# A gated mix of two attentions: maxima 90 slots ahead instead of 96, and two orders of halves in the projections

## The chip, the cores and the metric

One core of a Trainium2 chip runs the whole program. The time is device microseconds of one execution, the median of several runs. PE is the matrix engine, DVE the vector engine, ACT the scalar engine, POOL the general engine, SP the queue that issues most transfers.

## What is computed

`x` has 2048 rows of 512. Attention A is plain softmax attention with 32 heads of 16; attention B is causal-type attention within four chunks of 512 rows (the mask adds -1e9 where the key's row stands before the query's), mixed with a memory summed over the chunks before. A gate per row mixes both results. Cut to the core:

```python
qkv = split_heads(x @ wqkv)                                  # A
p = softmax(q @ k.T * scale); a = merge(p @ v) @ wo
for s in range(4):                                           # B, chunk by chunk
    p = softmax(qs @ ks.T * scale + mask); a_dot = p @ vs
    a_mem = (phi(qs) @ M) / (phi(qs) @ z + 1e-6)
    o[s] = sigmoid(beta) * a_mem + (1 - sigmoid(beta)) * a_dot
    M += phi(ks).T @ vs; z += phi(ks).sum()
b = merge(o) @ wo
out = g * a + (1 - g) * b        # g = sigmoid(x . gate_w)
```

## The kernel before

The program is written out in a fixed order for each engine; nothing is reordered later. It has a front and a slot loop.

**Front.** Projections are run in "slots" of twelve products of 128x512 (2 to 3 us of PE). Each operand is split into a high half (a rounded copy, ACT) and a low half (the rest, a subtraction on DVE or POOL), and a product is made of three half products. Work of the other engines is posted at one of four places in a slot: `post_at(n, place, f)` in slot n, `post(d, place, f)` d slots after the present one. What is posted at the same place runs in the order of posting. The slots are: 0 and 1 the values' first products (their additions, L550, follow on DVE, and the banks that they read come free); 2 and 3 take the split of the query weights (`wq8`, tile `qtmp` the low half, cast from `ph`); eight query tiles follow (`qk_tile`: copy L428, high half L429, low half L437, two stores to `qdA`); then the rest of the values; then the keys of two chunks in `k_pair`, seven slots with two accumulators each (copy L484, addition L491/L497/L502, high half L473, low half L477, stores to `kdA`), and again for the other two chunks; then values and, from slot 50 on, B's queries and keys with the memory (`tps`, `mps`, `num`, `den`).

**Maxima.** A score needs the row maximum of its query row in advance: the product is made once for the maximum alone (L242, into a bank `sm`), DVE reduces it over 512 columns (L275 for A; L290 with the mask for B), POOL combines the parts, PE transposes them (L232, `mt_ps`), ACT copies (L235, `mt`), and SP writes them as extra rows into the query tile (L238), so that the second product (L1065, `st`) gives scores less their maximum. A list `maxs` fixes the order of all 2368 maxima, with B's spread between A's. Those of the first `LEAD` slots are made in the front, four at a time (`some_max`), between projection tiles.

**Slot loop.** There are 2368 slots: 31 times a unit of A (64 slots) and one of B (10), then B31 and A31. A unit is four heads by 512 queries; A30 is the last A unit but one. Slot n makes one score (L1065), its exponential on ACT (L1088), and, `LEAD` slots ahead, one maximum. Three slots are a burst; at its end come products with values (L155, `ops`) or the transposition of maxima, whichever is due. A transposition becomes due 9 slots behind the last maximum of the next A unit or 12 slots ahead of the unit's own first score, whichever is first; two that are due together share one bank and one ACT copy. At the end, when no maxima are left (`wide`, `LEAD` - 6 slots), banks of the maxima serve scores too, six slots make a group, and output products fill PE (`fill`, up to 11 less the values taken): 24 for one block of rows, then the last chunk's (`blk`, `qclosed`, `kA` reused).

Of the kernel before, what the change touches and what calls it, by code (L numbers as in the profile page):

```python
# [31 lines left out]

SLOTS = {"A": 64, "B": 10}
NU = 32
LEAD = 96
BURST = 3
LATER = (2, 3)
MOST = 3
# [9 lines left out]
def gated_mix(ctx, tc, x, xT, wqkv, a_wo, b_wq, b_wk, b_wv, b_wo, beta, gate_w, out):  # L48
# [52 lines left out]
    def unit(side, k):  # L101
        return side, k % NG, k // NG
# [15 lines left out]
    for k in range(NU):  # L118
        mine = {u: iter(range(32)) for u in range(2)}
        bs = [k - 1] if 0 < k < NU - 1 else [k - 1, k] if k else []  # L120
        theirs = {r: [(unit("B", b), (r, i)) for b in bs for i in range(5)] for r in range(2)}
        start, apart = (33, (3, 3)) if k == 1 else (6, (9, 3)) if k < NU - 1 else (23, (3, 3))
        at_ = [next(m for m in range(len(maxs) + start, len(maxs) + start + 6) if m % 3 == 0)]
        while len(at_) < 10 * len(bs):
            at_.append(at_[-1] + apart[len(at_) % 2])
        for m in range(len(maxs), len(maxs) + 64 + 10 * len(bs)):
            r = (m + 1) % 2
            if m in at_ and bs:
                maxs.append(theirs[r].pop(0))
            else:  # L130
                maxs.append((unit("A", k), (r, next(mine[r]))))
        assert not theirs[0] and not theirs[1]
    last_max = {u: m for m, (u, _) in enumerate(maxs)}
    a_last = sorted(last_max["A", k % NG, k // NG] for k in range(NU))
    first_max = {u: m for m, (u, _) in reversed(list(enumerate(maxs)))}
    assert len(maxs) == nS and all(first[u] + LEAD - last_max[u] > 24 for u in units)

    qt, kt_ = {}, {}

    def raw(t):  # L140

        return t[:].bitcast(F32)
# [14 lines left out]
    def wait_early(n):  # L157

        loads_ = []
        for m in range(n + 1 + LEAD, n + 1 + BURST + LEAD):  # L160
            if m < nS:
# [47 lines left out]
    def finish_max(u):  # L209
        nm = pmt.pop(u)  # L210
        if u[0] == "A":
            pm, nm = nm, mp.tile([128, 4, 4], F32, tag="nm", name="nm")
            dm = mp.tile([128, 4, 4, 2], F32, tag="dm", name="dm")
            nc.gpsimd.tensor_sub(dm, pm[:, :, :, 2:4], pm[:, :, :, 0:2])  # L214
            nc.gpsimd.tensor_scalar_min(dm, dm, 0.0)
            nc.gpsimd.tensor_add(dm, dm, pm[:, :, :, 0:2])
            nc.gpsimd.tensor_sub(nm, dm[:, :, :, 1], dm[:, :, :, 0])
            nc.gpsimd.tensor_scalar_min(nm, nm, 0.0)
            nc.gpsimd.tensor_add(nm, nm, dm[:, :, :, 0])

        ms = mp.tile([128, 2, 2, 2, 4], F32R, tag="ms", name="ms")
        nv = nm.rearrange("p (r h) s -> p r h s", r=2)
        nc.gpsimd.tensor_copy(ms[:, :, 0], nv)  # L223
        nc.gpsimd.tensor_sub(ms[:, :, 1], nv, ms[:, :, 0].bitcast(F32))
        return ms
# [37 lines left out]
    def max_part(m, bank, b=None):  # L263
# [34 lines left out]
        if m == last_max[u]:  # L298
            def finish():

                due = min(e for e in a_last if e >= last_max[u]) + LATE_T
                late.append((min(due, first[u] + LEAD - 12), u, finish_max(u)))
            todo.append((m + 1, finish))

    def run_todo(m):

        for e in [e for e in todo if e[0] <= m]:
            todo.remove(e)
            e[1]()
# [22 lines left out]
    mnext = [0]  # L332
    with ExitStack() as p0:
# [22 lines left out]
        def f32(t):  # L356
            t = t[:]
            return t if t.dtype == F32 else t.bitcast(F32)
# [17 lines left out]
        def post(slots, place, f):  # L376
            posted.setdefault((now[0] + slots, place), []).append(f)
# [3 lines left out]
        def slot(products=(), chained=False):  # L381

            for place in range(4):
                for ps, l, r, start, stop in products[3 * place:3 * place + 3]:
                    nc.tensor.matmul(ps, l, r, start=start, stop=stop, skip_group_check=chained)  # L385
                for f in posted.pop((now[0], place), []):
                    f()
            now[0] += 1
# [6 lines left out]
        def post_at(n, place, f):  # L395
            posted.setdefault((n, place), []).append(f)
# [3 lines left out]
        def split(hi, lo, src, eng=V):  # L400

            nc.scalar.copy(hi, f32(src))
            eng.tensor_sub(lo, f32(src), f32(hi))
# [57 lines left out]
        def k_pair(xo, cs):  # L461

            X, Y, t = [None] * 2, [None] * 2, {}

            def out_tile(o, c, full, g, eng):
                q1 = wk.tile([128, CH], F32R, tag="q1", name="q1", bufs=3)
                q2 = wk.tile([128, CH], F32R, tag="q2", name="q2", bufs=3)

                def store(i, q):
                    nc.sync.dma_start(kd["A", o, cs[c]][16 * i:16 * i + 16].rearrange("d h t -> (d h) t"), raw(q))  # L470

                def high():
                    nc.scalar.copy(q1, full)  # L473
                    store(0, q1)

                def low():
                    eng.tensor_sub(q2, full, q1.bitcast(F32))  # L477
                    store(1, q2)
                post(*((0, 2) if g == 0 else (1, 0)), high)
                post(*((0, 3) if g == 0 else (1, 1)), low)  # L480

            def copy_x(g, tag):
                full = wk.tile([128, CH], F32, tag=tag, name="full", bufs=2)
                nc.scalar.copy(full, X[g])  # L484
                return full

            def done(p, g):
                if p == "p1":
                    t["1", g] = copy_x(g, "full")
                elif p == "p2":  # L490
                    V.tensor_add(t["1", g], Y[g], t["1", g])  # L491
                    out_tile(g, 0, t["1", g], g, V)
                elif p == "p6":
                    t["a", g] = copy_x(g, "am")
                elif p == "p5":
                    t["5", g] = copy_x(g, "full")
                    V.tensor_add(t["5", g], Y[g], t["5", g])  # L497
                    out_tile(2 + g, 1, t["5", g], g, V)
                elif p == "p3":
                    out_tile(2 + g, 0, copy_x(g, "full"), g, V)  # L500
                elif p == "p4":
                    V.tensor_add(t["a", g], Y[g], t["a", g])  # L502
                    out_tile(g, 1, t["a", g], g, V)
            for p, x, w in ORDER:
                x, w = xo[x], kops[w]
                prods = []
                for g in range(2):
                    if p == "p1":
                        X[g] = sm_bank()
                    elif p in ("p2", "p7"):  # L510
                        Y[g] = me_bank() if p == "p2" else pr_bank()
                    first = p in ("p1", "p2", "p7")
                    ps = X[g] if p in ("p1", "p6", "p5", "p3") else Y[g]
                    prods += [(ps, w[a][k][:, 128 * g:128 * g + 128], x[b][k], first and (a, b, k) == (1, 0, 0), (a, b, k) == (0, 0, 1))
                              for k in range(2) for a, b in PARTS]
                    post(0, 1 + 2 * g, lambda p=p, g=g: done(p, g))
                slot(prods, not first)
# [73 lines left out]
        def raw_ph():  # L591
            return [wk.tile([128, CH], F32, tag="ph", name="ph", bufs=4) for _ in range(4)]
# [23 lines left out]
        qraw = raw_ph()  # L616
# [3 lines left out]
        wq8 = (K4[1], Q4[0])  # L620
# [12 lines left out]
            op_split(vops["21" if k > 1 else "11"], vr[0][k // 2 * 2:], V, [k % 2])  # L633
            op_split(xo0["12" if k > 1 else "11"], x0[k // 2 * 2:], V, [k % 2])
        for k in range(KT):
            post_at(2, k, lambda k=k: split(wq8[0][k], wq8[1][k], qraw[k]))
            post_at(4, k, lambda k=k: op_split(xo0["22"] if k > 1 else a21, x1[k // 2 * 2:], V, [k % 2]))
        vb = (vr[0][0:2], vr[1][0:2], vr[0][2:4], vr[1][2:4])
        for k in range(2):
# [240 lines left out]
        def some_max():  # L880
            m = mnext[0]
            if m == LEAD:
                return
            loads(m + 3 + PRE)
            for i in range(4):
                max_part(m + i, lambda: me_sm.tile([128, CH], F32, tag="sm", name="sm"))
            run_todo(m + 3)
            mnext[0] += 4
            run_late(me_ps, "me", mnext[0])

        post_at(36, 1, lambda: loads(16))
# [8 lines left out]
        for n in range(32):  # L900
            if n in (14, 21, 29):
                post_at(S0 + n, 3, lambda c=n // 8: mem_q(c))
            elif n in (2, 4, 6, 8, 10, 12, 16, 18, 22, 24, 26):
                post_at(S0 + n, 3, some_max)

        def gates():
# [133 lines left out]

    wide = range(nS - LEAD + 2, nS - 4)
    assert wide.start % (2 * BURST) == wide.stop % (2 * BURST) == 0
# [115 lines left out]
    def octet(side, o, c, t0, vector=False):  # L1158
# [67 lines left out]
        if t0 is not None:  # L1226

            t0 += max([e + 2 - LEAD - t0 - ts[1] for e in a_last if 0 <= e + 1 - LEAD - t0 - ts[1] < 12], default=0)
        for n, f in zip(ts, (load, factors, send, factor, scale, store)):
# [117 lines left out]
    n = 0  # L1347
    while n < nS or queue or beside or filled[0] < len(fill):
# [4 lines left out]
        m = n + LEAD  # L1353
# [81 lines left out]
```

## Time and profile before

| | us |
|---|---|
| median of 3 runs (1738.92 to 1739.48) | 1738.96 |
| the profiled execution | 1738.98 |
| its span, first to last instruction | 1737.10 |
| front, to the first score | 272.7 |
| slots with maxima | 1389.2 |
| slots without maxima, to the last score | 51.5 |
| behind the last score | 23.8 |

Busy shares of the span: PE 100%, DVE 93%, ACT 83%, POOL 41%. PE's records are pipelined and their ends are modelled, so its share does not tell what it could still take; what it does is read from the starts of its rows. In the lines of the profile, `L242` is line 242 of the kernel, `sm<-kA,qA` says what is written from what, `x4` that four such instructions are merged, and `[0.84 <-DVE vs L550]` that the engine was idle 0.84 us until that instruction was done.

### The profile page before, as it was taken

The numbers are of one execution on the slowest core, as the hardware profiler recorded it, in microseconds if no ns is written. First come the engines' busy times: TensorE is split into PE (matmuls) and PEld (weight loads), VectorE is DVE, ScalarE is ACT, GpSimd is POOL, SyncE is SP. The second block draws the span as 40 slices with busy tenths as digits, with TensorE's granted clock in tenths as the row PEclk, the third lists the DMA queues.
The fourth block names the chain that finished last, engine by engine and source line by source line (L and its number), as shares of the span: only waits on it lengthen the run. The fifth ranks groups of instructions, "written<-read, shape, count | busy, mean of one in ns | idle before, by whom it ended". The sixth has DMA issues, their size and how long they took to land.

```text
span 1737.1 us, 41522 instructions
## 1 busy us (share of the span) xinstructions
PE 1729.1 (100%) x15157; PEld 875.5 (50%) x15157; DVE 1608.8 (93%) x3376; ACT 1439.9 (83%) x2774; POOL 706.8 (41%) x964
## 2 busy tenths in 40 slices
PE   9999999999999999999999999999999999999998
PEld 7877775444444444444444444444444444444444
DVE  7777987999999999999999999999999999999931
ACT  6543667888888888888888888888888888888884
POOL 1022544233353437444535353435354353435442
PEclk9999999999999999999999999999999999999999
DMA  7679887435453446454444453445444444444542
GB/s 246 193 241 238 303 278 218 112 93 156 116 159 102 142 124 175 132 141 125 137 138 143 133 148 122 134 140 139 141 123 149 131 141 113 144 119 147 149 152 63
DMA packets 168651, 264.97 MB, mean 153 GB/s; under 512 B 39512, under 2 KB 80760, under 8 KB 168448
## 3 DMA queue, kind: packets, MB, share of 16 engines
q1 hardware_dynamic: 166720, 260.78, 50.5%
q8 instruction: 121, 1.98, 0.5%
q0 software_dynamic: 1440, 1.14, 0.3%
q14 instruction: 82, 0.67, 0.1%
q10 hardware_dynamic: 288, 0.39, 0.1%
HBM read 177.74 MB, written 83.25 MB: 150 GB/s over the span
## 4 chain that ended last, share of the span: by engine, by line
PE 97%; DVE 1%; DMA 1%; ACT 0%; SPq 0%; issue 0%; ACTq 0%; DVEq 0%
PE ops L155 40%; PE st L1065 28%; PE sm L242 14%; PE pr L385 9%; PE pair L385 2%; PE sm L155 2%; DMA u<-xT 0%; PE mt_ps L232 0%; PE tps L851 0%; PE sm L1065 0%; DVE pm L275 0%; DMA u<-x 0%; PE mps L865 0%; PE num L823 0%; PE den L827 0%
## 5 line engine op out<-in xcount | busy, mean ns | idle before, releaser
L1088 ACT ACTIVATE p<-st 128x512 f32<-128x512 f32 x2261 | 1190.7, 600 | 146.8 <-PE sm L242 93.3
L275 DVE TENSOR_REDUCE pm<-sm 128x1 f32<-128x512 f32 x2048 | 1276.2, 682 | 8.3 <-PE sm L242 7.6
L242 PE MATMUL sm<-kA,qA 48*128 48x512 f32 x2048 | 662.2, 424 | 0.0
L1065 PE MATMUL st<-qA,kA 50*128 50x512 f32 x2014 | 655.9, 431 | 0.0
L155 PE MATMUL ops<-p,vA 128*17 128x256 f32 (+3 forms) x6360 | 552.2, 445 | 0.0
L1065 PEld LDWEIGHTS st<-qA,kA 50*128 50x128 f32 x2014 | 326.9, 185 | 423.4 <-ACT p L1088 379.7
L242 PEld LDWEIGHTS sm<-kA,qA 48*128 48x128 f32 x2048 | 337.8, 185 | 11.0 <-issue 4.2
L1189 POOL TENSOR_TENSOR rcp<-rec,minus 128x32 f32<-128x32 f32 x43 | 234.8, 5461 | 75.8 <-DMA rec<-dend 71.2
L290 DVE CUSTOM_DVE_ANT_0 rest<-sm,mask 128x128 f32<-128x128 f32 (+3 forms) x512 | 246.5, 481 | 0.0
L155 PEld LDWEIGHTS ops<-p,vA 128*17 128x17 f32 x6360 | 129.1, 96 | 215.7 <-issue 184.5
L1069 POOL TENSOR_SCALAR_AFFINE_SELECT p<-p 128x512 f32<-128x512 f32 x128 | 79.6, 638 | 267.6 <-ACT p L1088 263.1
L242 PE MATMUL sm<-kB,qB 48*128 48x128 f32 (+3 forms) x512 | 166.1, 384 | 0.0
L1065 PE MATMUL st<-qB,kB 50*128 50x512 f32 (+1 forms) x495 | 105.3, 329 | 0.3 <-ACT mt L235 0.3
L385 PE MATMUL pr<-u,u 128*128 128x512 f32 x392 | 101.4, 397 | 0.0
L1065 PEld LDWEIGHTS st<-qB,kB 50*128 50x128 f32 x495 | 68.5, 186 | 62.2 <-ACT p L1088 50.4
L155 PE MATMUL ops<-p,vB 128*17 128x128 f32 (+3 forms) x1504 | 88.3, 350 | 0.0
L385 PEld LDWEIGHTS pr<-u,u 128*128 128x128 f32 x392 | 71.8, 188 | 19.0 <-ACT u L834 2.5
L242 PEld LDWEIGHTS sm<-kB,qB 48*128 48x128 f32 x512 | 79.9, 184 | 0.0
L214 POOL TENSOR_TENSOR dm<-pm 128x32 f32<-128x32 f32 x32 | 7.8, 245 | 170.9 <-DVE pm L275 170.9
L434 POOL TENSOR_SCALAR mn<-full 128x512 f32<-128x512 f32 x24 | 39.0, 1625 | 53.8 <-ACT full L428 53.7
L223 POOL CAST ms<-pm 128x16 fp32r<-128x16 f32 x32 | 6.3, 198 | 127.5 <-DVE pm L290 127.5
L1205 POOL TENSOR_TENSOR v<-v,inv 128x512 f32<-128x512 f32 x31 | 39.8, 1284 | 28.7 <-DMA inv<-rdA 21.7
(227 smaller groups left out, 1422.5 us busy)
## 6 DMA issues: line engine op xcount, KB each, us to landing
kA<-kdA SPq DMA_DIRECT2D x256, 128.0 KB
vA<-vdA SPq DMA_DIRECT2D x31, 544.0 KB
kA<-kdA SPq DMA_DIRECT2D x256, 64.0 KB
kB<-kdB SPq DMA_DIRECT2D x192, 64.0 KB
qB<-qdB SPq DMA_DIRECT2D x192, 64.0 KB
kdA<-q SPq DMA_DIRECT2D x32, 256.0 KB
qA<-qdA SPq DMA_DIRECT2D x64, 128.0 KB
qdB<-q SPq DMA_DIRECT2D x32, 256.0 KB
```

Of the source, the lines that this page charges most:

```text
L155: behind[0] = nc.tensor.matmul(*args, **kw)
L214: nc.gpsimd.tensor_sub(dm, pm[:, :, :, 2:4], pm[:, :, :, 0:2])
L242: nc.tensor.matmul(ps[:, n0:n0 + n], rows(qt[u][:, :, s * 128:(s + 1) * 128], h, 48), rows(k[:, :, k0:k0 + n], h, 48), start=True, stop=True)
L275: nc.vector.tensor_reduce(pm[:, h, s, kc:kc + 1], ps, axis=AX.X, op=ALU.max, negate=True)
L290: nc.vector.tensor_tensor_reduce(out=tri["rest"][:, 0:w], in0=ps[:, n0:n0 + w], in1=tri["mask"][:, CH - w:], scale=-1.0, scalar=3.0e38, op ...
L385: nc.tensor.matmul(ps, l, r, start=start, stop=stop, skip_group_check=chained)
L434: nc.gpsimd.tensor_scalar_min(ph["mn"], full, 0.0)
L1065: nc.tensor.matmul(ps[:, n0:n0 + CH - q0], rows(k[:, :, b * 128:(b + 1) * 128], h, 50), rows(q[:, :, q0:], h, 50), start=True, stop=True)
L1069: nc.gpsimd.affine_select(out=x, in_=x, pattern=[[0, 4], [1, 128]], base=0, channel_multiplier=-1, compare_op=ALU.is_ge, fill=0.0)
L1088: nc.scalar.activation(p[:, h], ps, AF.Exp, scale=SCALE)
L1189: eng.tensor_tensor(r, rec, minus, op=ALU.pow)
L1205: eng.tensor_mul(k["v"], k["v"], k["inv"])
```

## The change

Four edits: the lead of the maxima falls from 96 to 90 slots, with B0's and the last B units' places in the list moved by six so that they meet the same slots as before; the front makes 90 maxima in 23 calls, the last one of two, instead of 96 in 24 (the calls in slots 60 and 62 become one in 61); the split of the third and fourth query weight moves from slot 2 to slot 3; and in `k_pair` the high half is made one place later, behind the next accumulator's copy, and the low half behind it.

```diff
-LEAD = 96
+LEAD = 90
...
-        start, apart = (33, (3, 3)) if k == 1 else (6, (9, 3)) if k < NU - 1 else (23, (3, 3))
+        start, apart = (27, (3, 3)) if k == 1 else (6, (9, 3)) if k < NU - 1 else (17, (3, 3))
...
-                post(*((0, 2) if g == 0 else (1, 0)), high)
-                post(*((0, 3) if g == 0 else (1, 1)), low)
+                post(*((0, 3) if g == 0 else (1, 2)), high)
+                post(*((1, 0) if g == 0 else (1, 3)), low)
...
-            post_at(2, k, lambda k=k: split(wq8[0][k], wq8[1][k], qraw[k]))
+            post_at(2 + k // 2, k, lambda k=k: split(wq8[0][k], wq8[1][k], qraw[k]))
...
-            for i in range(4):
+            for i in range(min(4, LEAD - m)):
                 max_part(m + i, lambda: me_sm.tile([128, CH], F32, tag="sm", name="sm"))
-            run_todo(m + 3)
-            mnext[0] += 4
+            run_todo(min(m + 3, LEAD - 1))
+            mnext[0] = min(m + 4, LEAD)
...
-            elif n in (2, 4, 6, 8, 10, 12, 16, 18, 22, 24, 26):
+            elif n in (2, 4, 6, 8, 11, 16, 18, 22, 24, 26):
```

On DVE at the end of the values' first products, the low halves of the query weights (`qtmp`) and the additions of values (`vs`):

```order
 L403 TENSOR_TENSOR u_257<-u_246,u_257 128x512
 L403 TENSOR_TENSOR qtmp<-ph,kA_194 128x512 x2
-L403 TENSOR_TENSOR qtmp<-ph,kA_195 128x512 x2
-L550 TENSOR_TENSOR vs<-pr,vt 128x8x4x16 x4
+L550 TENSOR_TENSOR vs<-pr,vt 128x8x4x16 x2
+L403 TENSOR_TENSOR qtmp<-ph,kA_195 128x512
+L550 TENSOR_TENSOR vs<-pr,vt 128x8x4x16
+L403 TENSOR_TENSOR qtmp<-ph,kA_195 128x512
+L550 TENSOR_TENSOR vs<-pr,vt 128x8x4x16
 L403 TENSOR_TENSOR kA_193<-u_247,kA_192 128x512 x2
```

The first addition stood behind four low halves and stands behind two; the other two low halves stand between additions.

On ACT in the first `k_pair`, copies of accumulators (`full<-pair`) and high halves (`q<-full`):

```order
 L402 CAST u_946<-ph 128x512 x2
-L484 COPY full<-pair 128x512
+L484 COPY full<-pair 128x512 x2
 L473 CAST q_954<-full 128x512
 L484 COPY full<-pair 128x512
-L473 CAST q_969<-full 128x512
+L402 CAST qtmp<-u_600 128x512 x2
+L473 CAST q_967<-full 128x512
+L484 COPY full<-pair 128x512
+L473 CAST q_981<-full 128x512
```

Both copies now stand ahead of the high half that stood between them.

On PE behind the last maximum, first of before, then of now: the groups of six scores (`st` and `sm` from `qA`, `qB`), values (`ops`), transpositions (`mt_ps`) and output products (`blk`):

```order
L1065 MATMUL st<-qA_21624,kA_195 128x512 x3
L1065 MATMUL sm_3246<-qA_21624,kA_195 128x512
L1065 MATMUL sm_3247<-qA_21624,kA_195 128x512
L1065 MATMUL sm_3248<-qA_21624,kA_195 128x512
L155 MATMUL ops<-p,vA 17x384 x4
L155 MATMUL sm_3245<-wA,blk 128x512 x3
L155 MATMUL sm_3245<-wB,blk 128x512 x3
L155 MATMUL sm_3245<-wA,blk 128x512 x2
L1065 MATMUL st<-qA_21624,kA_195 128x512 x3
```

```order
L1065 MATMUL st<-qA_21741,kA_195 128x512 x3
L1065 MATMUL sm_3228<-qA_21741,kA_195 128x512
L1065 MATMUL sm_3229<-qB_22558,kB_200 128x512
L1065 MATMUL sm_3230<-qB_22558,kB_200 128x512
L155 MATMUL ops<-p,vA 17x512 x4
L232 MATMUL mt_ps<-identf,ms 32x128
L1065 MATMUL st<-qB_22558,kB_200 128x512 x2
```

The group with eight output products is gone (its slots have maxima now), and what was the second group is the first, with one transposition instead of two; the other stands a group later. In the groups further on, by the same listing, the output products were 7, 9, 6, 6 and 6 in the third, fourth, sixth, eighth and fifteenth group and are 0, 11, 9, 9 and 7, and behind the last score six more are left. In the slot loop, B units' maxima are now transposed a burst or two ahead of A units', each with an ACT copy of 32 rows of its own: 64 copies in all instead of 33.

## The prediction

> **What bounds the kernel now.** I read first the busy time by stage, cut at the first score product (272.69 us), at the first stretch without maxima (1661.84) and at the last score (1713.34). Columns: stretch, its length, then busy us and count on PE, PEld, DVE, ACT, POOL, then granted clock, DMA share, GB/s.
>
> ```profile
> 0.00:272.69 272.69, 269.56 (x1656) 202.94 (x1657) 214.30 (x384) 153.35 (x280) 78.70 (x107) 1.00 0.79 251
> 272.69:1661.84 1389.15, 1389.14 (x13050) 635.25 (x13049) 1386.65 (x2977) 1238.18 (x2396) 598.17 (x824) 1.00 0.47 135
> 1661.84:1713.34 51.50, 51.20 (x366) 23.09 (x365) 2.77 (x4) 46.81 (x96) 29.43 (x35) 1.00 0.39 126
> 1713.34:1737.10 23.76, 19.24 (x91) 14.26 (x90) 5.06 (x11) 1.56 (x3) 0.46 (x1) 0.97 0.23 79
> ```
>
> The front has PE at work for 269.56 of 272.69 us and DVE only for 214.30: PE sets its pace. In the main loop DVE is busy 1386.65 of 1389.15, so the maxima set the pace; ACT has 151 us to spare. In the last stretch DVE does next to nothing, and PE and ACT share the bound. The clock is at full speed almost to the end, so it is no term here. Then the price of a maximum in the main loop, from the groups of DVE from 274.7 to 1661 and from its instructions in order of time.
>
> ```profile
> L275 DVE TENSOR_REDUCE pm<-sm 128x1 f32<-128x512 f32 x1952 | 1216.7, 682 | 0.7
> ```
> ```profile
> 1006.06 4.87 DVE L275 TENSOR_REDUCE pm<-sm 128x1 f32<-128x512 f32 x8
> ```
>
> One takes 0.68 us but they overlap: eight fill 4.87, so they follow each other at (4.87 - 0.68) / 7 = 0.60 us. In 1386 us DVE idled 0.7 us ahead of them.
>
> **The lead, in the main loop.** Six A maxima move from the front into the loop: 6 x 0.60 = +3.6 us, all on the path, since DVE has no idle time there. Nothing hides it. The loop then holds six more scores and their exponentials, which have ACT's spare time.
>
> **The lead, in the front.** Instructions of PE in order of time:
>
> ```profile
> 190.23 3.03 PE L385 MATMUL pr<-u,u 128*128 128x512 f32 x12
> 193.19 0.73 PE L242 MATMUL sm<-kA,qA 48*128 48x512 f32 x4
> 193.85 0.66 PE L851 MATMUL tps<-identf,ph 128*128 128x128 f32 x4
> ...
> 209.58 3.03 PE L385 MATMUL pr<-u,u 128*128 128x512 f32 x12
> 212.44 0.60 PE L851 MATMUL tps<-identf,ph 128*128 128x128 f32 x4
> ```
>
> From a projection tile to the transposes behind it takes 3.62 us with a call of four maxima between and 2.86 without: 0.76 for a call. Four products start within 0.66, so two of them are worth 0.33 at most, and two by two at the pace of other products about 0.25. One call and half of the last go: -1.0 us. It could be more only if PE waited there for DVE.
>
> **The lead, at the end.** PE again, one row at the start of each group of six slots:
>
> ```profile
> 1661.84 0.91 PE L1065 MATMUL st<-qA,kA 50*128 50x512 f32 x3
> ...
> 1665.84 0.73 PE L1065 MATMUL st<-qA,kA 50*128 50x512 f32 x3
> ...
> 1668.78 0.50 PE L1065 MATMUL st<-qB,kB 50*128 50x512 f32 x2
> ...
> 1673.11 0.73 PE L1065 MATMUL st<-qB,kB 50*128 50x256 f32 x5
> ...
> 1695.76 1.91 PE L155 MATMUL ops<-p,vA 128*17 128x512 f32 x16
> ...
> 1698.71 1.91 PE L155 MATMUL ops<-p,vA 128*17 128x512 f32 x16
> ...
> 1715.18 1.42 PE L155 MATMUL sm<-wB,qclosed 128*128 128x512 f32 x5
> ```
>
> The first group takes 4.00 us, the third 4.33; a group without output products takes 2.95, the pace of six exponentials. By the order the first group falls away (-4.0). The third loses its seven output products and becomes a group at ACT's pace (-1.38). The eight and seven output products of both come back: 2, 3, 3 and 1 in later groups and 6 behind the last score. Five of them take 1.42 us in the last row and twelve projection products 3.03 in the rows above, 0.25 each: 15 x 0.25 = +3.75. I count no cover for them (rival 3 does).
>
> One wait takes a place there. B31's maxima now reach its query rows through a transposition at the end of the second group, and its first score stands behind the third, which shrinks from 4.33 to 2.95. ACT's copy, SP's issue of two transfers, and for their landing the nearest transfer into SBUF (SP's issue, then DVE's wait):
>
> ```profile
> 1669.25 0.28 ACT L235 CAST mt<-mt_ps 64x128 fp32r<-64x128 f32 x1
> ```
> ```profile
> 1669.55 1.27 SPq L238 DMA_DIRECT2D qB<-mt  x2
> ...
> 1718.10 0.61 SPq L1170 DMA_DIRECT2D rec<-odA  x1
> ```
> ```profile
> 1720.41 0.35 DVE L1185 RECIPROCAL rec<-rec 128x32 f32<-128x32 f32 x1 [4.38 <-DMA rec<-odA]
> ```
>
> The copy stands behind the group's exponentials, so 0.3 + 1.27 + (1720.41 - 1718.71 =) 1.7 = 3.3 us follow them, against the 2.95 that ACT is busy with the next six. PE then transposes A31's maxima (0.3) before it scores again. So 0 (landing within 1 us) to +0.9 (after 2, as the copy ends 0.3 late); I take +0.5. The Trainium skill ("DMA: Bandwidth & Descriptors", section "Anatomy of one DMA") puts a fixed cost of about 2.0 us on each DMA, given there for the GpSimd path; by it this term would be an estimated +0.9 and the sum 0.4 higher, and the 1.7 here is nearer to that rule than to none. The end comes to -4.0 - 1.38 + 3.75 + 0.5 = -1.1.
>
> **Query weights.** PE, then DVE:
>
> ```profile
> 11.70 5.60 PE L385 MATMUL pr<-u,u 128*128 128x512 f32 x24
> 18.15 0.50 PE L385 MATMUL pr<-kA,qtmp 128*128 128x512 f32 x1 [0.84 <-DVE vs L550]
> ```
> ```profile
> 14.99 2.50 DVE L403 TENSOR_TENSOR qtmp<-ph,kA 128x512 fp32r<-128x512 f32 x4 [1.77 <-ACT kA L402]
> 17.41 2.48 DVE L550 TENSOR_TENSOR vs<-pr,vt 128x512 f32<-128x512 f32 x4
> ```
>
> The first query tile waits 0.84 us for a bank that the first addition frees, and that stands behind four low halves of 0.60. With two ahead it runs at 16.2 and is done at 16.9, before PE ends at 17.3. The third low half ends at 18.0, needed at 18.5; the fourth at 19.2, needed at about 19.2. So up to -0.84 at this place. But PE meets a wait further on that this does not move (SP, then ACT, then DVE):
>
> ```profile
> 44.99 1.86 SPq L407 DMA_DIRECT2D u<-xT  x4
> 46.95 0.85 SPq L425 DMA_DIRECT2D qdA<-q  x2
> ```
> ```profile
> 53.17 0.59 ACT L530 COPY vt<-pair 128x512 f32<-128x512 f32 x1 [4.17 <-DMA qdA<-q]
> ```
> ```profile
> 22.54 0.69 DVE L437 TENSOR_TENSOR q<-full,q 128x512 fp32r<-128x512 f32 x1 [0.25 <-ACT q L429]
> ...
> 43.91 0.68 DVE L437 TENSOR_TENSOR q<-full,q 128x512 fp32r<-128x512 f32 x1
> ```
>
> The copy of a bank that PE adds to next waited until 53.17 for the last query tile's store, which SP issued behind four loads and behind a low half that DVE, in arrears since 15 us, reached at 43.91. DVE's arrears shrink only by waits like the 0.25. So between -0.25 and -0.84 passes; I take -0.4, nearer to DVE's row.
>
> **Keys.** PE and ACT in the first pair of chunks:
>
> ```profile
> 78.60 4.24 PE L385 MATMUL pair<-qtmp,kA 128*128 128x512 f32 x18
> 83.08 1.66 PE L385 MATMUL pair<-qtmp,kA 128*128 128x512 f32 x6 [0.24 <-ACT full L484]
> ```
> ```profile
> 81.92 0.62 ACT L473 CAST q<-full 128x512 fp32r<-128x512 f32 x1 [0.95 <-DVE full L497]
> 82.44 0.58 ACT L484 COPY full<-pair 128x512 f32<-128x512 f32 x1
> ```
>
> PE waits 0.24 us for the copy at 82.44, which stands behind a high half that itself waits 0.95 for DVE. With the copy first the wait is gone: between -0.24 and -0.4 (24 products take 5.60 us and 18 take 4.24, so they start every 0.227; after 18 the next could start at 82.69 and does at 83.08). What is late next are the stores of keys, one place later in SP's queue, and the low halves on DVE ahead of the first maxima; that can cost as much. I take -0.3, bounds 0 and -0.4.
>
> **The transpositions.** Of A and B units' maxima, in the main loop now apart: 31 more ACT copies. PE's transposition of before, the first score on B's rows, and SP's issue between them:
>
> ```profile
> 1253.21 0.39 PE L232 MATMUL mt_ps<-identf,ms 128*32 128x128 f32 x4
> ...
> 1261.05 0.63 PE L1065 MATMUL st<-qB,kB 50*128 50x512 f32 x2
> ```
> ```profile
> 1253.95 1.40 SPq L238 DMA_DIRECT2D qB<-mt  x2
> ```
>
> 31 x 0.28 = 9 us of ACT (the copy's row above) lie in its 151 spare. B's rows are issued 0.74 us behind the transposition, 1.40 long, and 1.7 more to land: 3.8 of the 7.8 us that lie ahead of the first score. That lead shrinks by one burst (1.8 us): 6.0, still enough. I cost this at 0, covered by DVE's banks: four of them hold up to 2.4 us of maxima.
>
> **The sum.** Front -1.0 - 0.4 - 0.3 = -1.7; loop +3.6; end -1.1: +0.8 us. The profiled execution took 1738.98 us, its span 1737.10 and 1.88 around it; the median of the runs is 1738.96, the same. 1738.98 + 0.8 = 1739.8. The bounds: front -1.25 to -2.25, end -0.7 to -1.6, so 1738.7 to 1740.6 if all mechanisms are as said.
>
> **Rivals.** (1) The front's waits come back in full: both gaps close at their place and open at the next store (the ACT wait of 4.17 speaks for it, DVE's shrunken arrears against). Front -1.0 alone: 1738.98 + 3.6 - 1.0 - 1.1 = 1740.5.
>
> (2) Slower: each transposition apart takes a score bank from a burst, PE waits for ACT's copy, and DVE runs dry. The wait exists once at the end:
>
> ```profile
> 1669.58 0.44 PE L1065 MATMUL st<-qB,kB 50*128 50x384 f32 x1 [0.30 <-ACT mt L235]
> ```
>
> At 0.30 in 31 units it is 9.3 us: 1749.1. It decides from 0.09 us a unit (3.5 - 0.8 = 2.7 us over 31). Against it: the joint ones in the loop left DVE with 0.7 us of idle time in all.
>
> (3) Faster: the 15 output products that come back at the end run in PE's waits for ACT and cost nothing, B31's rows are in time, and the front gives all it can: 3.6 - 2.25 - 5.4 = -4.0, 1734.9. It needs PE to wait for ACT wherever products land; six of them land behind the last score, where ACT is busy 1.56 us of 23.76.
>
> (4) The low halves or copies do not move on the engine: excluded by the order, which shows them moved.
>
> **Chances.** Forecast 0.65, (1) 0.2, (2) 0.08, (3) 0.07. A measurement of this kernel tells about 0.2% (3.5 us) from no change: forecast and (1) are within it, (2) slower, (3) faster. The range takes in the bounds and (1) and some of what I have not seen on either side: 1737.2 to 1742.0.
>
> **What would show it.** The maxima in the loop 1958, DVE still without idle time, and the loop 3.6 us longer. The wait ahead of the first query tile gone, the ACT copy near 53 us still waiting for a store, PE's wait at 83 gone. Between the last maximum and the end some 74.6 instead of 75.7 us. 64 copies of transposed maxima on ACT, of 32 rows each, without a wait of DVE. The prediction is wrong if DVE idles in the loop, if a store or load in the front starts later and PE with it, or if the output products at the end are free.

## The result: slower by 19 us, and the profile after

The changed kernel takes 1758.28 us (median of four runs, 1757.53 to 1759.81), the kernel before 1738.94 in the same comparison: ratio 1.0116, 95% interval 1.0103 to 1.0129, 18 to 22 us. The prediction was 1739.8 and no change; it had given 0.08 to a slower kernel. The profiled execution took 1757.53, its span is 1755.81, 18.7 longer than before. The stages first, cut at the same places as before (length, busy us and count on PE, PEld, DVE, ACT, POOL, then granted clock, DMA share, GB/s):

```profile
0.00:270.00 270.00, 267.99 (x1649) 203.89 (x1649) 210.80 (x378) 152.75 (x280) 77.32 (x107) 1.00 0.80 254
270.00:1676.68 1406.68, 1403.37 (x13077) 642.77 (x13076) 1393.48 (x2983) 1247.05 (x2433) 603.74 (x828) 1.00 0.49 134
1676.68:1731.20 54.52, 50.78 (x341) 22.71 (x337) 2.77 (x4) 43.88 (x90) 25.51 (x31) 0.94 0.36 118
1731.20:1755.81 24.61, 20.57 (x97) 15.43 (x96) 5.07 (x11) 1.56 (x3) 0.00 (x0) 0.99 0.24 77
```

The front is 2.7 us shorter, the loop 17.5 longer, the two last stretches together 3.9 longer. DVE, busy but for 2.5 us of the loop before, is idle for 13.2 of it now, and the clock is no longer full in the third row. The group of A's maxima, then nine pairs of units in the middle of the loop (from one pair's transposition to that of the ninth behind it), first of now, then of before:

```profile
L275 DVE TENSOR_REDUCE pm<-sm 128x1 f32<-128x512 f32 x1958 | 1224.0, 691 | 6.7 <-PE sm L242 6.7
```
```profile
855.79:1263.75 407.96, 407.96 (x3821) 186.48 (x3817) 406.96 (x865) 364.33 (x712) 179.90 (x241) 1.00 0.49 135
```
```profile
847.01:1253.32 406.31, 406.31 (x3823) 184.98 (x3817) 406.11 (x865) 362.65 (x703) 180.80 (x242) 1.00 0.46 136
```

There are six more maxima in the loop (1958 for 1952), as predicted. DVE waited for PE ahead of them, 6.7 us against 0.7. Nine pairs with the same work (865 instructions on DVE in both, nine more on ACT) take 1.65 us longer: 0.18 a pair, 5.7 in 31. With the 3.6 of the six maxima, 17.5 leaves 8.2 us. Most of it stands in three places, by DVE's idle time there: 1.36 us at the pair near 490 us, 5.4 near 675 and 0.83 near 1632. In the trace of now, the question who waited for the line that sends maxima into the query tiles:

```profile
  PE ops L155: 4.8, 3
  PEld ops L155: 4.3, 2
```

Before, nobody waited for it. PE's three waits are 0.58 us near 490, 2.32 near 675 and 1.90 at the end. Near 1632 the rows were issued 3.1 us behind their copy, but PE's wait of 0.39 there is put down to an exponential, so late rows are not shown as the cause of that one. The pair near 675 us, ACT's copy and SP (an issue's start and length), then PE and DVE:

```profile
668.20 0.25 ACT L235 CAST mt<-mt_ps 32x128 fp32r<-32x128 f32 x1
```
```profile
668.59 1.29 SPq L1255 DMA_DIRECT2D blk<-hdB  x1
669.93 0.47 SPq L1018 DMA_DIRECT2D vA<-vdA  x1
670.49 1.76 SPq L177 DMA_DIRECT2D kA<-kdA  x4
672.35 1.43 SPq L238 DMA_DIRECT2D qB<-mt  x2
```
```profile
672.91 1.05 PE L155 MATMUL ops<-p,vA 128*17 128x384 f32 x14
676.28 0.44 PE L155 MATMUL ops<-p,vA 128*17 128x128 f32 x2 [2.32 <-DMA qB<-mt]
...
677.67 0.63 PE L1065 MATMUL st<-qB,kB 50*128 50x512 f32 x1
```
```profile
677.51 1.89 DVE L275 TENSOR_REDUCE pm<-sm 128x1 f32<-128x512 f32 x3 [2.94 <-PE sm L242]
680.50 1.89 DVE L275 TENSOR_REDUCE pm<-sm 128x1 f32<-128x512 f32 x3 [1.10 <-PE sm L242]
```

B's maxima are copied at 668.45, but SP issues their rows only at 672.35, behind the loads shown. They land 2.5 us behind the issue's end (673.78 to 676.25), and PE waits for them 2.32 us. It waits at a value product (`ops`), 1.4 us ahead of the first score on B's rows: the program hangs the waits for the next burst's transfers on the last product of the burst before. Before, the joint rows of this pair were issued at 667.82:

```profile
667.82 1.42 SPq L238 DMA_DIRECT2D qB<-mt  x2
```

The stall does not end with the wait. By the granted clock (the number behind PE's count):

```profile
673.90:676.28 2.38, 0.06 (x4) 1.00 0.98 272
676.28:679.60 3.32, 3.32 (x16) 0.53 0.73 253
679.60:683.00 3.40, 3.40 (x18) 0.50 0.20 57
683.00:690.00 7.00, 7.00 (x47) 0.98 0.56 179
```

Behind 2.38 us with almost no work PE runs at half its clock for 6.7 us. That is the 1.10 that DVE waits at 680.50, and 1.34 more behind it: 5.4 us of idle DVE at this pair, of which only 2.9 are the wait.

The end has the same two things, the rows of B31:

```profile
1680.41 0.44 PE L1065 MATMUL st<-qB,kB 50*128 50x384 f32 x1 [1.06 <-ACT mt L235]
...
1684.08 1.01 PE L155 MATMUL ops<-p,vA 128*17 128x512 f32 x1 [1.90 <-DMA qB<-mt]
```
```profile
1684.08:1692.00 7.92, 7.92 (x29) 4.67 (x31) 0.69 (x1) 3.31 (x7) 1.74 (x3) 0.61 0.93 339
```

PE waits 1.06 for ACT's copy, 1.90 for the transfer, and then works 7.9 us at 0.61 of its clock. In the front both of the predicted waits are gone and one is new:

```profile
17.57 0.39 PE L385 MATMUL pr<-kA,qtmp 128*128 128x512 f32 x1
...
97.41 0.96 PE L385 MATMUL pair<-qtmp,kA 128*128 128x512 f32 x3 [0.59 <-ACT full L484]
```

The new wait comes with the new orders: the kernel with them alone (e1 below) has it too, 0.58 us.

### The profile page after: what moved, and what is told of

The parts are those of the page before. It is cut to its first block, busy times and chain, and to the rows that moved or that the text cites. A ratio compares the mean times of both kernels' runs of the same rounds, so it can differ in the third digit from the quotient of the medians.

```text
span 1755.8 us, 41624 instructions
## 1 busy us (share of the span) xinstructions
PE 1742.7 (99%) x15157; PEld 884.8 (50%) x15157; DVE 1612.1 (92%) x3376; ACT 1445.2 (82%) x2805; POOL 706.6 (40%) x964
## 4 chain that ended last, share of the span: by engine, by line
PE 98%; DMA 1%; ACT 0%; DVE 0%; SPq 0%; issue 0%; POOL 0%; ACTq 0%; POOLq 0%; DVEq 0%
PE ops L155 40%; PE st L1065 27%; PE sm L242 14%; PE pr L385 11%; PE pair L385 2%; PE sm L155 2%; PE mt_ps L232 1%; DMA qB<-mt 1%; PE tps L851 0%; ACT p L1088 0%; PE sm L1065 0%; PE idle L346 0%; PE mps L865 0%; PE num L823 0%; PE den L827 0%
## 5 line engine op out<-in xcount | busy, mean ns | idle before, releaser
L155 PE MATMUL ops<-p,vA 128*17 128x256 f32 (+3 forms) x6360 | 558.7, 446 | 5.2 <-DMA qB<-mt 4.8
```

Of the source, the lines that this page charges most:

```text
L155: behind[0] = nc.tensor.matmul(*args, **kw)
```

## The experiments

Theory from this profile: the loss has three parts, all from B's transpositions standing apart and late: (T1) B's rows come late where SP is in arrears, and the clock falls behind the wait; (T2) an extra transposition costs by itself, 0.18 us a pair; (T3) B31's rows at the end. Rivals: the new orders in the front moved the transfers; the smaller lead costs by itself.

**Which edit.** Each half of the change alone.

```diff
 # e1: kernel before with both orders of halves, LEAD = 96
 # e2: changed kernel without them, LEAD = 90
```

> The kernel before with the two orders of halves alone (query weights, keys), lead 96. The first score of the changed kernel stands 2.69 us earlier than before (270.00 against 272.69). Theory: 1.0 of it is the call and a half of maxima, 1.7 the two orders, so the first score here at about 271.0 and the time at 1737.2. The terms of the prediction (0.4 + 0.3): 272.0 and 1738.2. If the waits come back further on: 272.7 and 1738.9.

> The changed kernel with the query weights and keys in the order of before: lead 90 alone. Theory that the loss sits in the slot loop and behind it, by late rows of B units: the three long stalls (at 493, 674 to 682 and 1632 us, 8 us of idle DVE in all) and the late rows of B31 stay, the front is 1.7 later, so about 1760. If the new order of the front moved transfers such that the stalls arise from it, they go: about 1750.

e1: 1737.91 against 1737.47, ratio 1.0002 (0.9993 to 1.0010): the two orders change nothing that can be measured, though in the one profile the first score stands 1.6 us earlier (271.10). e2: 1755.14, ratio 1.0107 (1.0088 to 1.0125), its six runs from 1750.90 to 1763.88. The lead alone makes the loss, and the loss varies from run to run by more than the kernel before does. The theory's 1760 was too high for the median, which lies halfway to the rival's 1750 (the front's order). What speaks against the rival is the profile: with the old order of the front the stalls at the first two of the three pairs are there (13.8 us of idle DVE in the loop), the third is not. That profile is of the slowest of the six runs, and its front is long too (first score at 275.59, with 1.84 us of PE's waiting at one place), so it tells that the stalls come without the new orders, not how large they are in a typical run.

**Rows earlier.** One number.

```diff
-                late.append((min(due, first[u] + LEAD - 12), u, finish_max(u)))
+                late.append((min(due, first[u] + LEAD - 18), u, finish_max(u)))
```

> The changed kernel with one number changed: B units' maxima are transposed 18 slots ahead of their first score instead of 12. Theory (late rows): rows land before PE's wait for them, the 8 us of stalls in the loop go, and so do about 5 us behind the last maximum: about 1745. What is left over before is then some 5 us in the loop (0.16 us a pair of units) besides the six maxima. If it is the mere number of transpositions, 64 instead of 33, or the smaller lead itself: no change, 1758.

1749.78, ratio 1.0069 (1.0056 to 1.0081): 8 us of the 19 come back. The end is 74.1 us (1671.67 to 1745.76), 5.5 less than with late rows, as expected. Stalls stay at two pairs. Near 480 us PE waits 0.64 us for keys of A, loaded late; B's rows of that pair are late too, but nobody waits for them. Near 675 the rows are still the cause, for a reason that was not foreseen (SP, then PE):

```profile
664.12 0.62 SPq L1170 DMA_DIRECT2D rec<-odB  x1
...
668.22 1.76 SPq L177 DMA_DIRECT2D kA<-kdA  x4
670.08 1.43 SPq L238 DMA_DIRECT2D qB<-mt  x2
```
```profile
674.31 0.38 PE L155 MATMUL ops<-p,vA 128*17 128x128 f32 x2 [2.32 <-DMA qB<-mt]
```

The transposition is two bursts earlier, and ACT's copy ends at 662.92, but the rows are issued 7.2 us behind it: SP works without a pause there, and its order has the loads ahead. An earlier due time does not help where the queue is the limit.

**A transposition apart, rows in time.** The same number in the kernel before.

> The kernel before (lead 96) with one number changed: B units' maxima are transposed 18 slots ahead of their first score, so apart from A's, 64 transpositions and ACT copies instead of 33, all rows in time. If a transposition of its own costs the 0.16 us a pair of units that the changed kernel's loop is slower between its stalls: 31 x 0.16 = 5.0, about 1743.9, with DVE idle 0.2 to 0.3 us at single places. If that loss comes from how six slots of lead move B's maxima against B's scores: 1738.9, within 0.5.

1745.70, ratio 1.0046 (1.0033 to 1.0059). PE waits for no rows in the loop, and still it is 6 us longer:

```profile
272.44:1667.29 1394.85, 1394.65 (x13045) 642.01 (x13048) 1391.08 (x2977) 1242.85 (x2426) 597.42 (x822) 1.00 0.47 135
```

Here and below the loop goes from the first score to the end of the last maximum on DVE. In the kernel before that is 272.69 to 1661.37, 1388.7 us, and the end behind it 75.7. So T2 holds: transpositions apart cost 1394.85 - 1388.7 = 6.2 us in the loop, and 1.7 at the end.

**What of a transposition costs.** In the kernel before, behind each joint one, at the end of the next burst, an idle one (e10), its product alone (e11), its copy alone (e12):

```diff
+            if again and again[0][0] < n:
+                us = again.pop(0)[1]
+                pt = st_ps.tile([128, CH], F32, tag="st", name="mt_ps")                      # e10, e11
+                nc.tensor.matmul(pt[:32, :128], us[0][2]..., identf, start=True, stop=True)  # e10, e11
+                nc.scalar.copy(mt2[:32], pt[:32, :128])                   # e10; e12 copies identf
-            if any(e[0] < m + 1 for e in late):
+            elif any(e[0] < m + 1 for e in late):
...
```

> The kernel before (lead 96, joint transpositions, rows at the same time) with one more transposition and ACT copy of 32 rows behind each joint one, at the end of the next burst, whose result nobody reads: 64 of each as in the changed kernel. If an extra transposition costs by itself (PE's 0.3 us, the score bank it takes, ACT's copy), the loop grows as with transpositions apart, by about 6 us: 1744 to 1745. If the 6 us there came from the different time of B's transposition: 1738.5.

> The kernel before with the idle transposition on PE behind each joint one, into a score bank, but without ACT's copy. With the copy the loop grew by 5.7 us and the time by 8.6. If the price is the score bank and PE's time (the next burst's first score gets the bank whose exponential runs one later): still +5 to +8.6, 1743.5 to 1747. If it is ACT's copy, 0.26 us late at the head of the next exponentials: 1738.5.

> The kernel before with an ACT copy of 32 rows (from a tile that is always there) behind each joint transposition, at the same place as in the kernel with idle transpositions, and no extra product on PE. If ACT's spare time in the loop covers a copy, as the prediction said: 1738.3, within 0.5. If the copy carries the cost: 31 x 0.19 to 0.28, 1744 to 1747.

e10: 1746.94, ratio 1.0049 (1.0035 to 1.0063). e11: 1746.55, ratio 1.0047 (1.0035 to 1.0060). e12: 1741.04, ratio 1.0016 (1.0007 to 1.0025). The loops of e11 and e12:

```profile
271.94:1665.88 1393.94, 1393.93 (x13103) 640.88 (x13106) 1389.12 (x2977) 1237.74 (x2395) 597.21 (x822) 1.00 0.47 135
```
```profile
272.33:1661.25 1388.92, 1388.91 (x13043) 634.95 (x13046) 1386.91 (x2977) 1242.32 (x2425) 598.48 (x822) 1.00 0.47 135
```

The copies add 0.2 us to the loop (1388.92 against 1388.7): ACT's spare time covers them, as the prediction said. e12's 2.7 us lie behind the last maximum (78.5 against 75.7), where its burst's output products are put off; none of the expectations had that part, and the same 2.7 to 3.0 are in e10 and e11. The products add 5.3 to the loop (5.7 with the copies): the loss comes with the product, which takes a score bank and PE's time. A burst of the kernel before and of e11, by the starts of the first scores around the transposition:

```profile
847.21 0.50 PE L1065 MATMUL st<-qA,kA 50*128 50x512 f32 x1
...
848.93 0.49 PE L1065 MATMUL st<-qA,kA 50*128 50x512 f32 x1
```
```profile
848.28 0.50 PE L1065 MATMUL st<-qA,kA 50*128 50x512 f32 x1
...
849.88 0.38 PE L1376 MATMUL mt_ps<-identf,ms 128*32 128x128 f32 x2
850.20 0.50 PE L1065 MATMUL st<-qA,kA 50*128 50x512 f32 x1
```

The same burst lasts 1.72 us without and 1.92 with the extra product, and PE does not make up for it. Counted one by one, the exponentials of e11 stand 1.07 us behind those of the kernel before ahead of this place and 1.27 behind it, and so on to the next pair. DVE follows 8 us later: its maxima stand 1.07 behind up to 856.50 and 1.28 from 857.11 on. That is 0.2 a pair. How much of the 0.2 is the bank and how much the product's time was not separated.

**Joint again, at lead 90.** A's maxima transposed sooner.

```diff
-LATE_T = 9
+LATE_T = 3
```

> The changed kernel (lead 90) with one number changed: A units' maxima are transposed 3 slots behind the last one instead of 9, so that 31 transpositions of A and B units are joint again, at the burst where B's stands in the changed kernel: 33 transpositions and copies instead of 64, B's rows no earlier. If transpositions apart cost the 0.18 us a pair of units by which the changed kernel's loop is slower between its stalls (407.96 against 406.31 in nine pairs), 31 x 0.18 = 5.7 go and the stalls at the pairs near 490, 675 and 1632 us stay: about 1752. If that loss is the shift by six slots itself: 1758. If POOL is not ready 6 slots sooner, PE waits for it at each transposition, and the time rises above 1758.

1787.36, ratio 1.0283 (1.0268 to 1.0297): the third outcome. POOL has not combined A's maxima yet. From the waits:

```profile
PEld mt_ps L232 <- POOL ms L224: 39.1, 32, 5.5
```

So at lead 90 the two cannot be joint: B's rows must leave before A's maxima are done. Whether joint ones would take away the 0.18 a pair it cannot tell.

**Rows by another queue.**

```diff
-                lands["score", u, r] = [nc.sync.dma_start(...)]
+                lands["score", u, r] = [(nc.scalar if u[0] == "B" else nc.sync).dma_start(...)]
```

> The changed kernel with one change: the two transfers of a B unit's rows (maxima into the query tile) are issued by ACT, right behind its copy, instead of by SP, where they stand behind loads and stores. Theory that SP's backlog makes the stalls: in the three pairs SP issued the rows 1.3, 3.9 and 3.3 us after the copy, everywhere else 0.03; issued at once they land 1 to 4 us sooner, and the stalls of 8 us in the loop go: about 1750 if ACT's issues cost nothing. If the loaded DMA engines alone delay the landing (share 1.02 at 672 to 676 us), the stalls stay: 1758. The price of the issues on ACT is unknown: SP needs 1.4 us for two; 31 of them on ACT lie in its 150 us to spare, and up to 20 us may pass.

1820.04, ratio 1.0473 (1.0453 to 1.0492), far outside what was expected. While ACT issues, it computes nothing:

```profile
680.04 1.31 ACTq L238 DMA_DIRECT2D qB<-mt  x2
681.39 3.04 ACT L1088 ACTIVATE p<-st 128x512 f32<-128x512 f32 x6 [1.39 <-DMA qB<-mt]
```

Exponentials waited so for 40.2 us in 29 pairs, and keys of A came late instead (up to 6.4 us of idle DVE at 688.8). The average of 150 us to spare was no cover for 1.3 us at one place. In its loop PE waits for no rows of B, but 19.8 us for keys of A, in nine places. So it does not settle T1.

**A longer lead.** `LEAD = 102`, 102 maxima in 26 calls of the front.

> The kernel before with the lead six slots longer, 102 instead of 96, in the front with 102 maxima in 26 calls; transpositions stay joint (31 of them), SP's issues of rows keep their cover. The terms of the prediction with their signs turned: loop -3.6, front +1.5 (a call and a half at 0.76 to 0.9, and a possible wait), end +0.6 to +4: about 1738 to 1740, within the noise of before. If a longer lead gains by itself (more slack of rows), it is below 1736; if transfers shift against each other as they do with 90, there are new stalls of DVE in the loop and it is above 1741.

1761.71, ratio 1.0136 (1.0122 to 1.0150): slower too. (The places of the last B units' maxima stay as they were here; the change had moved them.) One stall makes most of it, here for B's keys, then the clock:

```profile
1638.11 0.66 PE L1065 MATMUL st<-qB,kB 50*128 50x384 f32 x1 [6.72 <-DMA kB<-kdB]
```
```profile
1631.50:1638.10 6.60, 0.00 (x0) 0.02 (x1) 1.29 (x6) 1.06 (x2) 0.05 (x1) 0.71 0.51 151
1638.10:1645.00 6.90, 6.89 (x26) 4.63 (x26) 3.06 (x9) 2.77 (x5) 1.81 (x3) 0.50 0.47 110
1645.00:1652.00 7.00, 7.00 (x25) 3.47 (x26) 4.71 (x11) 4.37 (x10) 1.13 (x1) 0.50 0.00 0
1652.00:1660.00 8.00, 8.00 (x71) 3.58 (x67) 5.11 (x13) 4.64 (x11) 6.89 (x8) 0.62 0.09 33
```

Cut finer, the clock is at half from 1634.2 to 1658.2 us and full from then on. SP issued the keys at 1634.82, behind a store of a finished chunk (1631.35) ahead of which it had stood idle since 1627.0. So the lead need not be shorter to do harm. The reading is that six slots either way push loads (timed by maxima) against stores of finished chunks (timed by scores) in SP's fixed order; the next two runs test it for lead 90, none does for 102.

**The loads moved back.** The loads of rows 26 slots ahead instead of 20, at lead 90.

```diff
-PRE = 20
+PRE = 26
```

> The changed kernel with loads of query and key rows issued 26 slots ahead of their maxima instead of 20, so that they stand against the stores and loads of the finished chunks as they did with lead 96 (on SP the load of reciprocals, which waits for a store to land, is again behind the loads of A's queries and keys). Theory that the six slots pushed SP's loads behind such a wait and so delayed the rows: the stalls near 490, 675 and 1632 us shrink from 8 to under 3, about 1752. If not: 1758. Loads that now wait longer for a free tile could also stall PE elsewhere: above 1758.

1768.73, ratio 1.0176 (1.0162 to 1.0191). The stalls near 490 and 675 are gone, as T1 wants: B's rows are issued 0.70 us behind their transposition at both. But the front, whose loads this edit moves too, is 9.0 us longer than the changed kernel's (279.02), and at 1638 us a new stall of 6.1 us stands, for B's keys like that of the longer lead. So both remedies, where each does good:

```diff
-            loads(m + PRE)
+            loads(m + PRE + (6 if m < 2000 else 0))
...
-                late.append((min(due, first[u] + LEAD - 12), u, finish_max(u)))
+                late.append((min(due, first[u] + LEAD - 18), u, finish_max(u)))
```

> The changed kernel (lead 90) with both remedies together: B units' maxima transposed 18 slots ahead, and loads in the slot loop issued 26 slots ahead instead of 20, but only up to slot 2000 and not in the front. The theory adds up: kernel before 1738.3, six maxima in the loop +3.6, transpositions apart 31 x 0.17 = +5.3, the end -1.6 (74.1 against 75.7 in the run with the earlier rows), the front -0.7, no stalls at the pairs near 490 and 675: 1745. If the stalls do not come from SP's order of rows against loads, they stay and it is 1750; if transfers collide at another place, there is a new stall and it is above 1752.

1742.98, ratio 1.0029 (1.0020 to 1.0039): 15 of the 19 us come back, a little more than the theory's 1745. Loop and end:

```profile
269.19:1666.35 1397.16, 1397.08 (x13079) 641.44 (x13078) 1391.74 (x2983) 1246.20 (x2433) 602.39 (x826) 1.00 0.47 135
1666.35:1740.48 74.13, 68.24 (x438) 36.40 (x430) 7.84 (x16) 45.61 (x93) 25.70 (x32) 0.99 0.33 106
```

The loop is 8.5 us over the one before: 3.6 for the six maxima and 4.9. Behind its first 5 us, where all these kernels wait alike, DVE is nowhere idle for over 0.5 us, and nobody waits for rows. With e8 this shows T1, and with e3 T3. No version beat the kernel before.

## Why the prediction was wrong, step by step

**The transpositions, "I cost this at 0".** This step failed, in both of its halves. The sign that the prediction had named, DVE idle in the loop, is there: 13.2 us.

The first half was the time for B's rows: "3.8 of the 7.8 us that lie ahead of the first score. That lead shrinks by one burst (1.8 us): 6.0, still enough." The 7.8 was that of one pair; by the same reckoning other pairs of the kernel before have 6.4 and 7.5. At the undisturbed pairs of now 5.8 to 6.7 are left, and nobody waits: there the step held. It failed where SP is behind. The issue was assumed to follow the copy at once in all pairs, while at the pair near 675 us SP was 3.9 us in arrears; the landing took 2.5 us there where 1.7 was taken: 3.9 + 1.4 + 2.5 = 7.8 us from the copy to the landing. And the wait stands 1.4 us ahead of the score. The Trainium skill ("DMA: Bandwidth & Descriptors", section "Anatomy of one DMA") gives a fixed cost of about 2.0 us for a DMA, on the GpSimd path. That is nearer to the 2.5 than the 1.7 taken from a row, and still too short here. Nothing in the prediction asked what stands ahead of the rows in SP's queue at each pair; it looked at one pair.

The second half was the price of a transposition by itself. Rival 2 named a part of the mechanism, the score bank, and its 9.3 us are of the right order: 5.3 to 6.2 in the loop in e4, e10 and e11. Its price came from a wait for ACT's copy, though, and e11 loses as much without a copy. It got a chance of 0.08 since the joint ones "left DVE with 0.7 us of idle time in all". That DVE is always busy only shows that PE kept up, not by how much. The bursts around a transposition, 1.72 and 1.92 us long where DVE needs 3 x 0.60 = 1.80 for three maxima of A, could have warned that 0.2 more is not hidden. The part on ACT was right (e12).

**The clock, "no term here".** Wrong once PE waits: behind the two long waits it was 0.50 to 0.61 for 6.7 and 7.9 us.

**The end, -1.1.** One term was mis-sized: B31's late rows were given 0 to +0.9. The others add up as measured, though none was measured alone. With rows in time (e3, e9) the end takes 74.1, 0.5 less than the 74.6 predicted; with late rows it took 79.6 from the last maximum, and 1.06 + 1.90 of waits and the low clock make the difference.

**The loop's +3.6** fits: there are 1958 maxima, and e9's loop, 8.5 longer, has 3.2 left for them when its nine pairs (407.84 against 406.31, 0.17 a pair, 5.3 in 31) are taken off.

**The front, -1.7.** The profile shows -2.7, a little beyond the bound of -2.25, and the waits that the prediction named went; the ACT copy near 53 us still waits for a store, as it said. e1 does not resolve it by time: -1.2 to +1.7 us. Of the rivals, (1) can't be told from the forecast, (3) and (4) are out.

What the profiles add up to: front -2.7, six maxima +3.6, pairs +5.7, the rest of the loop, mostly the three stalls, +8.2, end +3.9: +18.7. One thing stays open. The nine pairs of the longer lead, with joint transpositions, also take 1.0 us more than before, so a part of the changed kernel's 1.65 may come from how the six slots place B's maxima against scores, and not from the second transposition; e5, meant to tell, ran into POOL. Counted one by one, the exponentials of now lose 0.15 to 0.22 us on those of before around the transpositions of each pair and nothing between the pairs, which fits the second transposition. But the longer lead, too, loses around the transpositions, 0.10 to 0.15 at two pairs of three.

## What to carry to other kernels

Where one queue issues loads, stores and small urgent transfers in a fixed order, a shift of one schedule against another has to be checked at every place where they meet, above all at the few where a chunk ends; one typical place is not enough. An engine that never idles does not show that the others have room: compare the lengths of their bursts. And a wait of 2 us on PE is priced with the slow clock that came behind it here.

## What was not expected of the hardware

Behind a pause of PE of 2.38 us its granted clock was at half for 6.7 us; behind one of 6.6 us (the longer lead) it was at half for 20. The Trainium skill ("TensorE: Matmul & The Clock Gate", section "Part 1: The HAM clock gate (the "warmup" mystery)") says that at least one window of idleness, about 3.4 us, brings half rate, and at least one of sustained work the full rate again. The trace agrees with the half rate, but here a shorter pause did, and the way back took 6.7 and 20 us. Two DMA issues on ACT's queue took 1.31 us in which its exponentials stood still.
